# A replanned order, in-place score products and another start in an attention and gated feed-forward block on one core

## The chip, the core and the metric

The kernel runs on one core of one Trainium2 chip. A core has TensorE (PE in the profile; its weight loads are PEld), VectorE (DVE), ScalarE (ACT), GpSimd (POOL) and SyncE (SP), which here issues all DMA transfers. The metric is device time in microseconds, the median of several executions.

## The reference

An input x of 2048 rows by 512 goes through an attention block with a compressed memory and then through a gated feed-forward block, both on a normalised input and both added to their input. Cut to what matters:

```python
# q, k, v: 32 heads of 16; the sequence is 4 segments of L = 512
for s in range(4):
    logits = einsum("bhqd,bhkd->bhqk", qs, ks) * 16**-0.5 + mask  # causal inside a segment
    a_dot = softmax(logits) @ vs
    pq = phi(qs)                               # t + 1 where t > 0, else exp(t)
    a_mem = (pq @ M) / (pq @ z + 1e-6)         # memory of the segments before
    outs.append(g * a_mem + (1 - g) * a_dot)   # g = sigmoid(beta) per head
    M = M + phi(ks).T @ vs ; z = z + phi(ks).sum over rows
h = x + concat(outs) @ wo
out = h + (gelu(ln(h) @ w_gate) * (ln(h) @ w_up)) @ w_down     # 1376 hidden columns
```

The two normalisations are over a row of 512, and everything is in float32.

## The kernel before

Large products are made from a high and a low part of each operand (three matrix products in place of one: high with high, high with low, low with high; `SPLIT`). So each operand that comes from a projection or from memory is split by an ACT copy (high) and a DVE or POOL subtraction (low).

The attention's work is cut into 16 units U: a chunk c of 8 heads in a segment s. A unit projects q and k (`qkv`), splits them, spreads them by DMA into the buffers `stq` and `stk`, updates the memory, and is then handled in two halves Q of 4 heads, 32 in all. `pass_a(Q)` computes the scores once to find each query row's largest score: 11 tiles of up to 512 columns go from PE into one of two PSUM banks (`PA`), and 16 DVE products (`tensor_tensor_reduce` with the mask, a custom operation in the profile, followed by a read of its accumulator) take the minimum of the negated scores. Their element-wise output is not used; it goes into a buffer `junk`. Widths are 128 (i + 1) columns for i = 3, 2, 1, 0, with four products each. The 16 columns of minima are transposed on PE and sent by DMA into a spare row of `stq`, so that the second scores come out with the maximum subtracted. `pass_b(Q)` computes those scores with the keys on the partitions, again into two banks (`PB`), ACT takes the exponential into `pt`, POOL clears what the mask hides, and PE sums the weighted values with products tiled by columns (four at a time).

The order is not written by hand. Every instruction is recorded with its engine, a duration, a priority and what it reads and writes; `Sched.run` then plays a list schedule on these estimates: among what could start within a small window, the lowest priority number goes first. Priorities are the unit's or half's number plus an offset from the table `DUE` (one list per kind of step: `q` projections, `a` and `b` the two passes, `p` the weighted sums, and so on). `LAT` is the time that the planner adds between an instruction's end on one engine and its consumer's start on another; `TAKEN` is the same for a buffer's return. Buffers come from pools (`Pool_`); a pool with `fifo=True` hands them out in the order of the program's text. What comes out is a fixed order of instructions for each engine; on the chip each engine runs through its order and waits by semaphores.

At the start, `ln1(0)` loads four row tiles and normalises them. While DVE finishes the statistics, 17 transposes whose result is unused keep PE at work; then 16 transposes bring the rows into four banks, ACT and DVE split them into `xt`, and the first projections of q and k (`project`) follow. With `ln1(1)`, the first units and their scores join.

After attention, `wo_seg` multiplies with wo and adds x, and the feed-forward block runs over 11 column tiles with products combined after Strassen's scheme (`ffn`, `down`). The change touches none of these functions.

Of the kernel before, what the change touches and what calls it, by code (L numbers as in the profile page):

```python
# [15 lines left out]
P = 128  # L16
D = 512
T = 2048
NSEG = 4
NCH = 4  # L20
ND = D // P
# [10 lines left out]


DUE = {
# [17 lines left out]
}  # L52


# [65 lines left out]
class Op:  # L120
# [2 lines left out]

LAT = {
    "PE": {"PE": 0.0, "ACT": 0.27, "DVE": 0.246, "POOL": 0.24, "SP": 0.25},
    "ACT": {"PE": 0.14, "ACT": 0.12, "DVE": 0.137, "POOL": 0.172, "SP": 0.12},
    "DVE": {"PE": 0.108, "ACT": 0.12, "DVE": 0.17, "POOL": 0.165, "SP": 0.12},
    "POOL": {"PE": 0.085, "ACT": 0.08, "DVE": 0.09, "POOL": 0.12, "SP": 0.12},  # L130
}
TAKEN = {"PE": 0.22, "ACT": 0.14, "DVE": 0.12, "POOL": 0.1}
DRAIN = 0.1


# [106 lines left out]
def infini_geglu(ctx: ExitStack, tc: tile.TileContext, x, wq, wk, wv, wo, beta,  # L242
# [8 lines left out]
    def sb(name, shape, dt=F32):  # L251
        return p0.tile(shape, dt, name=name)

    def many(name, n, shape, dt=F32):
        return [sb(f"{name}{i}", shape, dt) for i in range(n)]
# [14 lines left out]
        return S.op("POOL", dur, prio, fn, ins, outs, **k)  # L270

    def dma(prio, fn, ins, outs, kb=256, dur=None, **k):
        return S.op("SP", dur or (0.4 if kb == 256 else 0.68), prio, fn, ins, outs, lat=kb / 290, **k)

    def mm(n):
        return max(n / 2400 + 0.0133, 0.109)
# [34 lines left out]
    PACC = Pool_([], fifo=True)  # L311
    PGE = Pool_(many("ge", 1, [P, D]))
    PC = Pool_([])
    PPT = Pool_(many("pt", 2, [P, D]), then=PACC)
    PROW1 = Pool_(many("pt1", 9, [P, D]), then=PPT)
    PJ = Pool_(many("junk", 2, [P, D]), then=PC)
    PE_ = Pool_(many("e", 1, [P, D]), then=PC)
    PPQ = Pool_(many("pq", 1, [P, D]), then=PC)
    PPK = Pool_(many("pk", 1, [P, D]), then=PC)
    PPKN = Pool_(many("pkn", 1, [P, D]), then=PC)  # L320
    PPVS = Pool_(many("pvs", 1, [P, D]), then=PGE)
# [7 lines left out]
    PMB = Pool_(many("mb", 7, [P, 160]))  # L329
    PNM = Pool_(many("nm", 2, [P, 2, 2, 4]))  # L330
    PMM = Pool_(many("mm", 2, [P, 2, 2, 8], F32R))
    PMX = Pool_(many("mx", 2, [32, P]))
    PBN = Pool_(many("bn", 2, [P, 4, 6]))
    PMV = Pool_(many("mv", 2, [P, 4, 2]))
    PLN = Pool_(many("ln", 8, [P, 4]))

    ident = sb("ident", [P, P])
    amask = sb("amask", [P, D])
# [1 line left out]
    one = sb("one", [P, 1])  # L340
    gt = sb("gt", [P, 2, NCH])
    tick = sb("tick", [P, 1])
    o_dram = dram.tile([NSEG, 4, P, NCH, P], F32, name="o_dram")
    r_dram = dram.tile([16, 2, 8, D], F32, name="r_dram")
    pv_dram = dram.tile([16, 2, P, D], F32, name="pv_dram")
# [2 lines left out]
    vident, vamask, vmmask, vgt = (Val() for _ in range(4))  # L348


    vh = Val(PJ)
    vj = Val(PJ)


# [101 lines left out]
    def layer_norm(prio, rows, dst, off=False, keep=None, acq=None, done=(), behind=(), scratch=None):  # L456
# [37 lines left out]
        if done and not behind:  # L494

            wm = Val(PB)
            pe(17 * 0.227, prio, lambda: [nc.tensor.transpose(
                wm.t[0:24, 0:P], bn.t.rearrange("p t k -> p (t k)"), ident) for n in range(17)],
                [bn, vident], [wm])

        def g():
# [62 lines left out]
                    op1=OP.mult), [rows[t], mv, y], [rows[t]])  # L564
        if done and not behind:

            pts = [Val(PA if dc == 3 else PD) for dc in range(ND)]
            pe(4 * TR, prio, lambda: [nc.tensor.transpose(
                pts[dc].t[:, t * P:(t + 1) * P], rows[t].t[:, dc * P:(dc + 1) * P], ident)
                for t in range(4) for dc in range(ND)], [*rows, vident], pts, acq=dst)  # L570
            for dc in range(ND):
                split_psum(prio, pts[dc], dst[dc])
            return
# [47 lines left out]
            pe(3 * mm(D), prio, f, [w, XT[s][dc]], [pm], acq=acq)  # L621
        return pm

    def phi(prio, pm, pool_):

        e, r = Val(PE_), Val(pool_)
        act(D, prio, lambda: nc.scalar.activation(e.t, pm.t, AF.Relu, scale=-1.0), [pm], [e],
            acq=[r])
        act(D, prio, lambda: nc.scalar.activation(e.t, e.t, AF.Exp, scale=-1.0), [e], [e],
            src=0.092)  # L630
        dve(D, prio, lambda: nc.vector.scalar_tensor_tensor(
            r.t, pm.t, 0.0, e.t, op0=OP.max, op1=OP.add), [pm, e], [r])
        return r
# [31 lines left out]
    def qkv(U):  # L665
# [5 lines left out]
        moved = prio + DUE["d"][U]  # L671
        for Q in half:
            STQ[Q], STK[Q] = Val(PSQ), Val(PSK)
        for i in range(2):
            hl = Val(PHL)
            if U == 0:
                HL0.append(hl)
            pm = project(first + 0.1 * i, W[s // 2, c, i], s, [hl])
            sc = 0.25 if i == 0 else 1.0
            act(D, first, lambda pm=pm, hl=hl, sc=sc: nc.scalar.activation(  # L680
                hl.t[:, 0], pm.t, AF.Copy, scale=sc), [pm], [hl])
            dve(D, first, lambda pm=pm, hl=hl, sc=sc: nc.vector.scalar_tensor_tensor(  # L682
                hl.t[:, 1], pm.t, sc, hl.t[:, 0].bitcast(F32), op0=OP.mult, op1=OP.subtract),
                [pm], [hl])
            if i == 0 and s:
                PQ[U] = phi(first, pm, PPQ)
            if i == 1 and s < NSEG - 1:
                PQ[U, "k"] = phi(first, pm, PPK)
            for h, Q in enumerate(half):
                dst = (STQ, STK)[i][Q]  # L690
                zeros = (vq0, vk0)[i][Q:Q + 1]
                for r, part in enumerate(((0, 1, 0), (0, 0, 1))[i]):
                    if i == 0:
                        dma(moved + 0.2 + h, lambda dst=dst, r=r, part=part, h=h, hl=hl:
                            nc.sync.dma_start(dst.t[r:P:4].bitcast(F32),
                                              hl.t[64 * h:64 * h + 64, part].bitcast(F32)),
                            [hl] + zeros, [dst], kb=128, chain=True)
                        continue
                    for a in range(2):
                        dma(moved + 0.2 + h, lambda dst=dst, r=r, part=part, h=h, hl=hl, a=a:  # L700
                            nc.sync.dma_start(
                                dst.t[64 * a + r:64 * a + 64:4, :, a].bitcast(F32),
                                hl.t[64 * h + 32 * a:64 * h + 32 * a + 32, part].bitcast(F32)),
                            [hl] + zeros, [dst], kb=64, chain=True)
                if i == 0 and Q >= len(stq_t):
                    dma(moved + 0.2 + h, lambda dst=dst: nc.sync.dma_start(
                        dst.t[3:P:32].bitcast(F32), amask[0:16, 0:2 * P]), [vamask], [dst],
                        kb=16, chain=True)
# [74 lines left out]
    def pass_a(Q):  # L783
# [4 lines left out]
        def part(heads, i):  # L788
# [12 lines left out]
            m = mm(2 * w if i < 2 else w)  # L801
            pe(m * len(heads) / 2 if i < 2 else m, prio, f, [sq, sk], [sa], acq=[nm], tail=m)
            for k, (a, p) in enumerate(heads):
                junk = Val(PJ)

                def g(k=k, a=a, p=p, junk=junk):
                    nc.vector.tensor_tensor_reduce(  # L807
                        out=junk.t[:, :w], in0=sa.t[:, k * w:(k + 1) * w], in1=amask[:, D - w:],
                        op0=OP.add, op1=OP.min, scale=-1.0, scalar=BIG,
                        accum_out=nm.t[:, a, p, i:i + 1])  # L810
                dve(w, prio, g, [sa, vamask], [junk, nm], chain=True)
        for i in (3, 2):
            for n in range(4):
                part([(n % 2, n // 2)], i)
# [23 lines left out]
    def pass_b(Q):  # L838
# [55 lines left out]
        def accum(kbs, last):  # L894
            def f():
                for kb in kbs:
                    for n in range(4):
# [4 lines left out]
                                         e.t[:, lo:lo + D - kb * P], start=kb == 0,  # L902
                                         stop=last and kb == kbs[-1],
                                         tile_position=(0, 32 * n), skip_group_check=True)
            pe(sum(0.02 + 0.86 * (4 - kb) / 4 for kb in kbs), Q + 1.122 + DUE["p"][Q], f,
               [va, *dict.fromkeys(pt[n, kb][0] for kb in kbs for n in range(4))], [pv], head=0.03,
               tail=0.02, mode="c")
        for n in range(4):
# [395 lines left out]
```

## Time and profile before

| | |
|---|---|
| median of 3 runs | 831.09 us (830.61 to 831.82) |
| the profiled execution | 830.79 us, of which the span of the profile is 829.1 us |
| PE | busy 805.0 us, 97% of the span |
| DVE, ACT, POOL | 74%, 68%, 58% busy |
| granted PE clock | 1.00 in the mean of the span |

"L807" is line 807 of the kernel before. In a group's row stand the line, the engine, the operation, output and inputs by the program's names, shapes, the count, then total busy time and the mean duration of one in ns, then the idle time of the engine in front of these instructions and what ended it. Products on PE overlap in the pipeline, so their mean duration (390 ns for 512 columns) is longer than their distance, and a busy PE can still lose time in small gaps.

### The profile page before, as it was taken

The page shows a single profiled execution, that of the slowest core. Times are in us where ns is not written, and L with a number is a line of the kernel's source. Part 1 is how long each engine was busy: PE and PEld are TensorE (multiplying, and loading weights), DVE is VectorE, ACT ScalarE, POOL GpSimd, SP SyncE. Part 2 cuts the span into 40 slices and gives each one's busy share as a digit, 9 for nine tenths or more (in the row PEclk, how much of TensorE's full clock was granted, in tenths as well). Part 3 has the DMA queues.
Part 4 walks back from the last instruction along what each step waited for, and adds up shares of the span by engine and source line. Part 5 has one row for each costly group of instructions (what it writes and reads, how often), then busy time and mean ns, then how long its engine had stood idle before and what let it go on. Part 6 is the DMA issues. An engine that isn't in the chain of part 4 may idle for free.

```text
span 829.1 us, 15346 instructions
## 1 busy us (share of the span) xinstructions
PE 805.0 (97%) x4709; PEld 623.6 (75%) x4709; DVE 612.0 (74%) x1831; ACT 563.5 (68%) x1127; POOL 484.2 (58%) x719
## 2 busy tenths in 40 slices
PE   5999999999999999999999999999999999999998
PEld 4877767777777677776667677777888887788886
DVE  7888678788895878888896874676568856756565
ACT  6877868689988768776776862787467464545551
POOL 7533433444445444544736895788697686778750
PEclk9999999999999999999999999999999999999999
DMA  6543534565456564556554665531111341212102
GB/s 229 148 133 94 153 108 130 151 182 155 118 156 177 159 154 119 154 152 169 165 163 144 200 200 166 164 115 48 55 55 48 95 162 51 65 39 63 51 1 102
DMA packets 71750, 103.52 MB, mean 125 GB/s; under 512 B 14324, under 2 KB 24884, under 8 KB 71668
## 3 DMA queue, kind: packets, MB, share of 16 engines
q1 hardware_dynamic: 71668, 102.54, 42.6%
q8 instruction: 37, 0.61, 0.3%
q14 instruction: 45, 0.37, 0.2%
HBM read 54.92 MB, written 21.43 MB: 92 GB/s over the span
## 4 chain that ended last, share of the span: by engine, by line
PE 77%; DVE 10%; ACT 4%; issue 3%; POOL 3%; DMA 2%; SPq 1%; ACTq 0%; POOLq 0%; DVEq 0%
PE bank L1145 19%; PE bank L1206 14%; PE bank L619 8%; PE bank L797 8%; PE bank L869 7%; PE bank L900 7%; PE bank L973 4%; PE bank L648 4%; DVE junk L807 3%; ACT pt L876 1%; PE bank L726 1%; POOL raw L1122 1%; PE bank L772 1%; PE bank L579 1%; DVE hl L682 1%
## 5 line engine op out<-in xcount | busy, mean ns | idle before, releaser
L807 DVE CUSTOM_DVE_ANT_0 junk<-bank,amask 128x256 f32<-128x256 f32 (+3 forms) x512 | 228.3, 485 | 43.4 <-PE bank L797 40.3
L879 POOL TENSOR_SCALAR_AFFINE_SELECT pt<-pt 128x128 f32<-128x128 f32 (+2 forms) x352 | 118.8, 346 | 191.6 <-ACT pt L876 183.5
L876 ACT ACTIVATE pt<-bank 128x512 f32<-128x512 f32 (+1 forms) x352 | 181.4, 560 | 42.8 <-PE bank L869 36.4
L797 PE MATMUL bank<-stk,stq 128*128 128x512 f32 (+2 forms) x384 | 128.1, 377 | 4.3 <-DVE nm L807 3.9
L869 PE MATMUL bank<-stq,stk 128*128 128x384 f32 (+2 forms) x384 | 110.8, 351 | 1.7 <-ACT pt L876 1.4
L619 PE MATMUL bank<-xt,w 128*128 128x512 f32 x384 | 108.4, 394 | 1.1 <-DVE xt L589 1.1
L1211 DVE TENSOR_TENSOR pt<-pt,bank 128x512 f32<-128x512 f32 x96 | 65.0, 685 | 41.7 <-PE bank L1206 40.1
L797 PEld LDWEIGHTS bank<-stk,stq 128*128 128x128 f32 x384 | 68.6, 188 | 28.4 <-DVE nm L807 13.8
L869 PEld LDWEIGHTS bank<-stq,stk 128*128 128x128 f32 x384 | 67.3, 188 | 19.9 <-ACT pt L876 8.3
L619 PEld LDWEIGHTS bank<-xt,w 128*128 128x128 f32 x384 | 70.4, 188 | 12.5 <-DVE xt L589 1.3
L900 PE MATMUL bank<-pt,vaug 128*32 128x512 f32 (+3 forms) x1024 | 77.0, 436 | 0.0
L900 PEld LDWEIGHTS bank<-pt,vaug 128*32 128x32 f32 x1024 | 28.9, 109 | 39.1 <-issue 30.2
L648 PE MATMUL bank<-wv,xt 128*128 128x256 f32 x384 | 54.9, 283 | 0.0
L648 PEld LDWEIGHTS bank<-wv,xt 128*128 128x128 f32 x384 | 52.2, 189 | 1.8 <-issue 0.2
L1145 PE MATMUL bank<-xt,w 128*128 128x512 f32 (+1 forms) x186 | 51.2, 391 | 0.4 <-DVE n L1171 0.4
L1115 POOL TENSOR_TENSOR w<-raw,w 128x512 fp32r<-128x512 f32 (+3 forms) x37 | 42.0, 1137 | 6.8 <-ACT w L1113 6.6
L435 POOL TENSOR_TENSOR w<-raw,w 128x512 fp32r<-128x512 f32 (+1 forms) x23 | 29.7, 1291 | 22.3 <-ACT w L430 22.1
L807 DVE DVE_READ_ACCUMULATOR2_ANT nm<- 128x1 f32 x512 | 42.0, 82 | 0.0
L1145 PEld LDWEIGHTS bank<-xt,w 128*128 128x128 f32 (+1 forms) x186 | 34.3, 186 | 8.9 <-ACT ge L1163 0.8
L1145 PE MATMUL bank<-stk,w 128*128 128x512 f32 (+1 forms) x138 | 38.8, 390 | 0.0
L1122 POOL TENSOR_TENSOR raw<-raw,raw 128x256 f32<-128x256 f32 (+1 forms) x44 | 35.2, 799 | 2.9
L1122 POOL TENSOR_TENSOR raw<-raw 128x256 f32<-128x256 f32 (+1 forms) x44 | 33.6, 765 | 1.8
(298 smaller groups left out, 1798.5 us busy)
## 6 DMA issues: line engine op xcount, KB each, us to landing
stq<-hl SPq DMA_DIRECT2D x96, 128.0 KB
stk<-hl SPq DMA_DIRECT2D x192, 64.0 KB
pv_dram<-pvs SPq DMA_DIRECT2D x32, 256.0 KB
r<-r_dram SPq DMA_DIRECT2D x28, 256.0 KB
row<-x SPq DMA_DIRECT2D x24, 256.0 KB
raw<-wg SPq DMA_DIRECT2D x20, 256.0 KB
raw<-wu SPq DMA_DIRECT2D x20, 256.0 KB
raw<-wd SPq DMA_DIRECT2D x20, 256.0 KB
```

Of the source, the lines that this page charges most:

```text
L619: nc.tensor.matmul(pm.t, w.t[:, wi, dc * P:(dc + 1) * P], XT[s][dc].t[:, xi, :], start=dc == 0 and n == 0, stop=dc == ND - 1 and n == 2)
L648: nc.tensor.matmul(pm.t[:, 256 * t:256 * t + 256], XT[s][dc].t[:, xi, t0:t0 + P], whl[wi].t[:, h, 256 * (dc % 2):256 * (dc % 2) + 256], st ...
L797: nc.tensor.matmul(sa.t[:, k * w:(k + n) * w].rearrange("x (n w) -> x n w", n=n), sq.t[:, p, i * P:(i + 1) * P], sk.t[:, p, a:a + n, 0:w], ...
L807: nc.vector.tensor_tensor_reduce(out=junk.t[:, :w], in0=sa.t[:, k * w:(k + 1) * w], in1=amask[:, D - w:], op0=OP.add, op1=OP.min, scale=-1 ...
L869: nc.tensor.matmul(sc.t[:, lo:lo + D - q0], sk.t[:, p, a, q0:q0 + P], sq.t[:, p, q0:D], start=True, stop=True)
L876: act(w, prio, lambda: nc.scalar.activation(e.t[:, :w], sc.t[:, :w], AF.Exp), [sc], [e])
L879: nc.gpsimd.affine_select(v, v, pattern=pat + [[1, P]], compare_op=OP.is_ge, fill=0.0, base=0, channel_multiplier=-1)
L900: nc.tensor.matmul(pv.t[32 * n:32 * n + 32, kb * P:D], va.t[:, kb, 17 * j:17 * j + 32], e.t[:, lo:lo + D - kb * P], start=kb == 0, stop=la ...
L1122: pool(0.14 + 2.13e-3 * h, prio, lambda: nc.gpsimd.tensor_tensor(d.t[:, d0:d0 + h], a.t[:, a0:a0 + h], c.t[:, c0:c0 + h], op=o), ins, [d])
L1145: nc.tensor.matmul(dst.t[:w], v.t[:, wi, c0 + j * w:c0 + (j + 1) * w], b[bk][j].t[:, xi, :], start=first and j == 0 and n == 0, stop=j == ...
L1206: nc.tensor.matmul(pm.t, HH[p, f, s][hi].t[:w, t * P:(t + 1) * P], v.t[:w, wi, :], start=f == fl[0] and n == 0, stop=f == fl[-1] and n == 2)
L1211: dve(D, prio, lambda a=a, pm=pm: nc.vector.tensor_tensor(a.t, a.t, pm.t, op=OP.add), [pm], [a])
```

## The change

- In `pass_a`, products of width 512 and 384 (i = 3 and 2) write their unused output over the scores that they read, in the bank. Those of width 256 and 128 write into one small buffer, `aside`. One `junk` buffer goes, and with it the planner's reservation of one per product.
- The number of buffers changes: two for phi(q) in place of one, one transposed maximum (`mx`) in place of two, six small normalisation buffers in place of eight; `pt` buffers are handed out in the text's order; buffers of phi are reserved before the projection.
- The planner's numbers: hand-overs from ACT, DVE and POOL to PE 0.40 us longer, returns of buffers from ACT and DVE 0.10 us longer, the weighted sums' durations and small DMAs' durations changed, and all of `DUE` replaced. These move instructions, and cost nothing by themselves.
- The start: 12 unused transposes in place of 17; the transposed rows go to two banks of `PA`, one of `PB` and one of the three others, and the first two projections (`project_two`) run together, per slice with the high part of x times both weight parts for q and k first, and then the low part.

Each score pass has two banks before and after. Line numbers after the change are higher: the row-maximum products are L825 (L807 before), their scores L817 (L797), pass B's scores L887 and L880 (L869 and L862), its exponential L894 (L876), the weighted sums L918 (L900), projections L621 and, for the first two, L633 (L619).

```diff
 DUE = {
-    "q": [-2.625, -0.25, 3.5, 2.5, 1.75, 1.625, -0.25, 0.875, 0.375, 0.625, 1.75, 1.75, 1.75, 1.625, 3.5, 1],
+    "q": [-4, -4, 1.75, 2.5, 4, -3.75, 2.375, 1.25, 2.25, 4, 1.875, 3.875, 3.5, -3.5, 0.75, 4],
...
-    "w": [0.25, -0.375, -3.5, 3.125],
-    "l": [0, 0, 0.125, -0.25],
+    "w": [1.875, 0.875, -3.375, 4],
+    "l": [0, 0, -1.625, 0.375],
...
-    "ACT": {"PE": 0.14, "ACT": 0.12, "DVE": 0.137, "POOL": 0.172, "SP": 0.12},
-    "DVE": {"PE": 0.108, "ACT": 0.12, "DVE": 0.17, "POOL": 0.165, "SP": 0.12},
-    "POOL": {"PE": 0.085, "ACT": 0.08, "DVE": 0.09, "POOL": 0.12, "SP": 0.12},
+    "ACT": {"PE": 0.54, "ACT": 0.12, "DVE": 0.137, "POOL": 0.172, "SP": 0.12},
+    "DVE": {"PE": 0.508, "ACT": 0.12, "DVE": 0.17, "POOL": 0.165, "SP": 0.12},
+    "POOL": {"PE": 0.485, "ACT": 0.08, "DVE": 0.09, "POOL": 0.12, "SP": 0.12},
...
-TAKEN = {"PE": 0.22, "ACT": 0.14, "DVE": 0.12, "POOL": 0.1}
+TAKEN = {"PE": 0.22, "ACT": 0.24, "DVE": 0.22, "POOL": 0.1}
...
-    PPT = Pool_(many("pt", 2, [P, D]), then=PACC)
+    PPT = Pool_(many("pt", 2, [P, D]), fifo=True, then=PACC)
...
-    PJ = Pool_(many("junk", 2, [P, D]), then=PC)
+    PJ = Pool_(many("junk", 1, [P, D]), then=PC)
...
-    PPQ = Pool_(many("pq", 1, [P, D]), then=PC)
+    PPQ = Pool_(many("pq", 2, [P, D]), then=PC)
...
-    PMX = Pool_(many("mx", 2, [32, P]))
+    PMX = Pool_(many("mx", 1, [32, P]))
...
-            pe(17 * 0.227, prio, lambda: [nc.tensor.transpose(
-                wm.t[0:24, 0:P], bn.t.rearrange("p t k -> p (t k)"), ident) for n in range(17)],
+            pe(12 * 0.21, prio, lambda: [nc.tensor.transpose(
+                wm.t[0:24, 0:P], bn.t.rearrange("p t k -> p (t k)"), ident) for n in range(12)],
...
-            pts = [Val(PA if dc == 3 else PD) for dc in range(ND)]
+            pts = [Val(pool_) for pool_ in ((PA, PA, PB, PD) if not behind else (PD, PD, PD, PA))]
...
+    def project_two(prio, w, s, acq):
+        pm = [Val(PD), Val(PD)]
+        for dc in range(ND):
+            def f(dc=dc):
+                for n, (i, wi, xi) in enumerate((i, wi, xi) for wis, xi in (((0, 1), 0), ((0,), 1))
+                                                for i in range(2) for wi in wis):
+                    nc.tensor.matmul(pm[i].t, w[i].t[:, wi, dc * P:(dc + 1) * P], XT[s][dc].t[:, xi, :],
+                                     start=dc == 0 and n in (0, 2), stop=dc == ND - 1 and n > 3)
+            pe(6 * mm(D), prio, f, [*w, XT[s][dc]], pm, acq=acq if dc == 0 else [])
+        return pm
...
             for k, (a, p) in enumerate(heads):
-                junk = Val(PJ)
-
-                def g(k=k, a=a, p=p, junk=junk):
+                def g(k=k, a=a, p=p):
                     nc.vector.tensor_tensor_reduce(
-                        out=junk.t[:, :w], in0=sa.t[:, k * w:(k + 1) * w], in1=amask[:, D - w:],
+                        out=sa.t[:, :w] if i > 1 else aside[:, k * w % 256:k * w % 256 + w], in0=sa.t[:, k * w:(k + 1) * w], in1=amask[:, D - w:],
                         op0=OP.add, op1=OP.min, scale=-1.0, scalar=BIG,
                         accum_out=nm.t[:, a, p, i:i + 1])
-                dve(w, prio, g, [sa, vamask], [junk, nm], chain=True)
+                dve(w, prio, g, [sa, vamask], [nm], chain=True)
...
-            pe(sum(0.02 + 0.86 * (4 - kb) / 4 for kb in kbs), Q + 1.122 + DUE["p"][Q], f,
+            pe(sum(0.735 * (4 - kb) / 4 for kb in kbs) + (0.17 if last else 0.06), Q + 1.122 + DUE["p"][Q], f,
```

More of the change, by code (lines that the diff above doesn't have):

```diff
@@ L272, in dma @@
     def dma(prio, fn, ins, outs, kb=256, dur=None, **k):
-        return S.op("SP", dur or (0.4 if kb == 256 else 0.68), prio, fn, ins, outs, lat=kb / 290, **k)
+        return S.op("SP", dur or (0.4 if kb == 256 else 0.64), prio, fn, ins, outs, lat=kb / 290, **k)
     def mm(n):
@@ L331, in infini_geglu @@
     PMM = Pool_(many("mm", 2, [P, 2, 2, 8], F32R))
[L332 removed]
+    PMX = Pool_(many("mx", 1, [32, P]))
     PBN = Pool_(many("bn", 2, [P, 4, 6]))
     PMV = Pool_(many("mv", 2, [P, 4, 2]))
[L335 removed]
+    PLN = Pool_(many("ln", 6, [P, 4]))
     ident = sb("ident", [P, P])
@@ L342, in infini_geglu @@
     tick = sb("tick", [P, 1])
+    aside = sb("aside", [P, 2 * P])
     o_dram = dram.tile([NSEG, 4, P, NCH, P], F32, name="o_dram")
@@ L348, in infini_geglu @@
     vident, vamask, vmmask, vgt = (Val() for _ in range(4))
-    vh = Val(PJ)
+    vh = Val(PE_)
     vj = Val(PJ)
@@ L622, in project, with phi @@
         return pm
-    def phi(prio, pm, pool_):
-        e, r = Val(PE_), Val(pool_)
+    def project_two(prio, w, s, acq):
[8 more added lines that the diff above has]
+        return pm
+    def phi(prio, pm, r):
+        e = Val(PE_)
         act(D, prio, lambda: nc.scalar.activation(e.t, pm.t, AF.Relu, scale=-1.0), [pm], [e],
@@ L673, in qkv @@
             STQ[Q], STK[Q] = Val(PSQ), Val(PSK)
+        hls = Val(PHL), Val(PHL)
+        if U == 0:
+            first_two = project_two(first, [W[0, 0, 0], W[0, 0, 1]], 0, hls)
         for i in range(2):
-            hl = Val(PHL)
+            hl = hls[i]
             if U == 0:
                 HL0.append(hl)
-            pm = project(first + 0.1 * i, W[s // 2, c, i], s, [hl])
+            if i == 0 and s:
+                PQ[U] = Val(PPQ)
+            if i == 1 and s < NSEG - 1:
+                PQ[U, "k"] = Val(PPK)
+            r = PQ.get((U, (U, "k"))[i])
+            pm = project(first + 0.1 * i, W[s // 2, c, i], s, [hl] + ([r] if r else [])) if U else first_two[i]
             sc = 0.25 if i == 0 else 1.0
@@ L684, in qkv @@
                 [pm], [hl])
[L685 to L688, printed above, removed]
+            if r:
+                phi(first, pm, r)
             for h, Q in enumerate(half):
```

28 rows, old and new, of the table DUE are left out of this document.

## The prediction

> **What bounds the kernel now.** First the head of the profile page, for the engine that is full.
>
> ```profile
> span 829.1 us, 15346 instructions
> PE 805.0 (97%) x4709; PEld 623.6 (75%) x4709; DVE 612.0 (74%) x1831; ACT 563.5 (68%) x1127; POOL 484.2 (58%) x719
> ```
>
> TensorE (PE) is busy for 805.0 of 829.1 us, so 24.1 us is all that it idles outright, and the change takes no matrix product away: in the order of the built programs the same 4,072 products stand in both, beside 17 warm-up transposes before and 12 after. What can change is the start, and the small waits inside the "busy" 97%. The windows view tells where these are.
>
> ```profile
> core 0: us, PE busy (x) PEld busy (x) DVE busy (x) ACT busy (x) POOL busy (x), PEclk, DMA share, GB/s
> 20.00:100.00 80.00, 78.57 (x548) 61.49 (x548) 65.29 (x258) 65.51 (x137) 33.74 (x67) 1.00 0.49 132
> 100.00:400.00 300.00, 295.20 (x2106) 222.18 (x2108) 242.23 (x955) 235.58 (x501) 136.09 (x297) 1.00 0.54 149
> 400.00:480.00 80.00, 76.13 (x489) 52.63 (x482) 66.03 (x215) 60.09 (x121) 53.22 (x88) 1.00 0.58 177
> ...
> 560.00:829.00 269.00, 264.36 (x1173) 215.08 (x1172) 172.81 (x266) 141.00 (x254) 185.52 (x179) 1.00 0.21 64
> ```
>
> The feed-forward part (from about 480 us) loses almost nothing: 1.7% idle in its last window, and that holds the output's way out behind the last product. Attention loses PE time in crumbs, with VectorE (DVE) at about 81% of each of its stretches. The view of waits says for whom PE's weight loads (PEld) and its products wait.
>
> ```profile
> PEld bank L900 <- issue: 30.2, 121, 0.4
> PEld bank L797 <- DVE nm L807: 13.8, 32, 1.7
> PEld bank L869 <- ACT pt L876: 8.3, 24, 1.0
> ...
> PEld bank L900 <- POOL pt L879: 7.0, 28, 0.4
> ...
> PEld bank L830 <- DVE pk L631: 2.4, 3, 1.6
> PEld bank L862 <- ACT pt L876: 2.3, 5, 0.9
> PEld bank L830 <- DVE mm L826: 1.6, 4, 0.5
> ...
> PE bank L797 <- DVE nm L807: 3.9, 8, 0.8
> PE bank L869 <- ACT pt L876: 1.4, 3, 0.5
> ```
>
> The columns are total us, times, longest. Score products (L797, L869, L862) wait for a bank whose last reader, a row-maximum product on DVE or an exponential on ACT, isn't done. [...]
>
> **The start.** The chain that ended last, over the first 20 us:
>
> ```profile
> 7.61 3.58 PE bank L497 x17
> 11.19 1.43 PE bank L568 x13
> ...
> 13.27 0.70 DVE xt L589
> ...
> 14.02 5.08 PE bank L619 x21
> ```
>
> and from the timeline and the view of line 497 (durations min/median/max in ns, first and last start):
>
> ```profile
> 9.80 1.45 DVE L533 TENSOR_SCALAR pt<-pt,mv,ln 128x512 f32<-128x512 f32 x3
> 9.92 0.82 ACT L545 ACTIVATE pt<-pt,ln,ln 128x512 f32<-128x512 f32 x1 [0.52 <-DVE ln L539]
> ...
> 12.64 2.07 ACT L588 ACTIVATE xt<-bank 128x512 fp32r<-128x512 f32 x4 [1.91 <-PE bank L568]
> ...
> L497 PE MATMUL bank<-ident,bn x17: 273/421/421, 7.6 to 10.9; 128*24 128x128 f32 x17
> ```
>
> The 17 warm-ups take 3.58 / 17 = 0.21 us each, and hold the real transposes (L568, 1.43 / 13 = 0.11 us each) until about 11.1. The first normalised row is there at 9.80 + 0.48 = 10.3, the third at 11.25, ACT's fourth at 10.74. With 12 warm-ups PE is free by 7.6 + 12 x 0.21 = 10.1, so the last eight transposes hang on the third row: 11.25 + 0.1 + 8 x 0.11 = 12.2, against 11.19 + 1.43 = 12.6. That is 0.4 us. Then the projection: before, its first product waits for the low part (L589, done at 13.97), because it uses the bank that L589 reads and PE takes a slice's three products together. After, two free banks and the order "high part times both weight parts, for q and k, then the low part" let PE start behind the first L588, at about 12.2 + 0.6 + 0.1 = 12.9 instead of 14.0. From there 24 products at 5.08 / 21 = 0.24 us set the pace: per slice four high products take 0.96 us, longer than L588's 2.07 / 4 = 0.52. Start and end of the projections come 1.1 us earlier. Some may be lost to the value weights, split by ACT and POOL; some is won since SP's order now sends the first head's six key parts without a weight load between them. I take **-1.2** (ends 0 and -2).
>
> **The wide products over their scores.** 256 of the 512 row-maximum products (512 and 384 columns) now write into the bank they read; the narrow ones write into one buffer. No run here shows this operation so; the nearest rows are an add from bank to bank and the same add into on-chip memory:
>
> ```profile
> L807 DVE CUSTOM_DVE_ANT_0 junk<-bank,amask 128x512 f32<-128x512 f32 x128 | 85.9, 683 | 13.1 <-PE bank L797 12.3
> L807 DVE CUSTOM_DVE_ANT_0 junk<-bank,amask 128x384 f32<-128x384 f32 x128 | 67.7, 551 | 20.7 <-PE bank L797 19.6
> ...
> L1157 DVE TENSOR_TENSOR bank<-vaug,bank 128x512 f32<-128x512 f32 x22 | 15.2, 693 | 11.7 <-PE bank L1145 8.4 <-ACT vaug L1152 3.2
> ...
> L1157 DVE TENSOR_TENSOR vaug<-vaug,bank 128x512 f32<-128x512 f32 x9 | 6.2, 687 | 1.3 <-PE bank L1145 1.3
> ```
>
> 693 - 687 = 6 ns more each: 256 x 6 ns = 1.5 us of DVE, spread under its 19% idle time. Some 32 of 512 products are waited for, so PE sees 1.5 x 32 / 512 = **+0.1** us; at -6 to +60 ns each it would be -0.1 to +1. The bank is released by the same instruction as before. The freed buffer goes to a second phi(q) buffer; one transposed-maximum buffer instead of two costs nothing, since its DMA leaves before the next maximum, on average 13 us of PE work later.
>
> **The turns of PE.** The order has 65 runs of column-tiled products after, 62 before, so 129 turns against 123: 6 x 0.25 (30.2 / 121) = **+1.5** us (ends 0 and 2.4).
>
> **The new order.** The waits that a better order can remove are those on DVE and ACT: 13.8 + 8.3 + 2.4 + 2.3 + 1.6 = 28.4 us in 68 waits, 0.42 us each. Not all is lost time, as the product in front still streams while a load waits; PE's own rows show 3.9 + 1.4 = 5.3 us idle outright. Between 5 and 28 us I take the middle, 17 us. How much goes is read from the order, with each product at its pace in the trace, as PE work between two instructions. The distance at which a score bank is reused was under 1.4 us (product 0.68, two hand-overs and the rest) for 126 of 351 pass-A tiles and 175 of 351 pass-B tiles; after, 100 and 140, a fifth fewer. From a maximum's transpose to the first pass-B product the median goes from 7.5 to 10.1 us, from the key transpose to the memory update from 1.7 to 2.9, from the last score product to the last weighted sum from 2.6 to 2.95. All grow while PE's work stays the same, so no length is paid for it. The planner's hand-overs to PE got 0.40 us longer, as long as the mean wait. A fifth by the counts, more by the mean: I take a third of 17 us, **-6** (ends 0 and -17, and above nothing by the second rival).
>
> Sum: -1.2 + 0.1 + 1.5 - 6 = -5.6 us. The profiled execution took 830.8 us (its span 829.1 and 1.7 around it), 0.3 under the median of 831.1; the forecast stands to the median: 831.1 - 5.6 = **825.5 us**.
>
> **Rivals.**
> 1. *The waits only move* (no real change): other tiles wait in place of these, as the longest singles (1.7, 1.6, 1.0 us) come from a full DVE queue, which a margin doesn't empty. Left are -1.2 + 0.1 + 1.5 = +0.4: 831.5 us. For: DVE has the same work. Against: all distances grew.
> 2. *DVE falls behind in clumps* (slower). With DVE's instructions at their durations, the seven fullest stretches of 20 us of PE work in attention carry 27, 27, 25, 24, 24, 23 and 22 us after, 25, 25, 24, 23, 23, 22 and 22 before: 8 us more. If PE has other work ready for half of it, that is +4 us, and with the other terms 831.1 + 4 + 0.4 = 835.5 us. It decides where a stretch holds over 23 us of DVE work, more than DVE can do in the 21.5 us that PE then really takes; I count six after, four before. Against: PE's work between two maxima spreads no worse (standard deviation 3.0 against 2.9 us).
> 3. *All waits under 0.4 us go*, as every margin holds: about 13 of the 17 us; 831.1 - 13 + 0.4 = 818.5 us, and 814.5 if all 17 go.
> 4. *The clock is late.* PE's pace went from 0.21 to 0.11 us a transpose within the last warm-ups (the shortest of them has 273 ns, the others 421), so after about 3.2 us, at 10.8. Twelve last 2.5 us, and a pause of 0.2 us follows. If full pace then comes one such stretch later, at about 14, 16 transposes at +0.1 and five products at +0.23 us cost 1.6 + 1.1 = 2.7: 828.2 us with the rest as forecast. For keeping the time: the transposes that follow keep PE at work across 10.8. [...]
>
> **How the numbers follow.** About 0.2% (1.7 us) is what a measurement of this kernel can tell from no change. Chances: forecast (821 to 829.4) 0.48, rival 3 0.12, rival 4 0.08, rival 1 0.10, rival 2 0.22. Faster are the forecast and rivals 3 and 4, 0.68; same is rival 1 with its edge towards slower, 0.09; slower 0.23. The range holds the forecast's ends, rivals 1, 3 and 4 down to 815, and the nearer half of rival 2: 815 to 836. The forecast's own range is 820 to 829.
>
> **What would show it.** Right: first projection product near 12.9 us; the waits of L797's and L869's successors on DVE and ACT at two thirds of 22.1 us together; wide products at 690 and 557 ns; L900's successor with some 127 "issue" waits. Wrong: projections starting at 13.5 or later at 0.4 us a product (the clock); those waits unchanged (rival 1); DVE's idle time before the wide products, 13.1 + 20.7 = 33.8 us now, down to 24 with PE waiting more (rival 2).

## The result and the profile after

The changed kernel takes **835.57 us** (834.05 to 835.94) against 831.09 us (830.48 to 831.82): slower by 4.5 us, a ratio of 1.0051 with a 95% interval of 1.0037 to 1.0066. The forecast was 825.5.

First the head of the page of the changed kernel, then rows of its view of waits (total us, times, longest).

```profile
span 833.7 us, 15303 instructions
PE 810.5 (97%) x4704; PEld 625.8 (75%) x4704; DVE 619.1 (74%) x1831; ACT 564.4 (68%) x1127; POOL 484.2 (58%) x719
```

```profile
PEld bank L918 <- issue: 34.1, 136, 0.4
PEld bank L817 <- DVE nm L825: 15.3, 43, 1.0
PEld bank L918 <- POOL pt L897: 5.9, 20, 0.6
PEld bank L887 <- ACT pt L894: 5.0, 12, 0.9
PEld bank L880 <- ACT pt L894: 2.8, 6, 1.3
PE bank L817 <- DVE nm L825: 3.1, 8, 0.5
```

PE's outright idle time did not grow (24.1 us before, 833.7 - 810.5 = 23.2 now): what was lost lies inside its busy share, where a weight load waits while the product in front still counts as busy. The waits of pass B on ACT did get shorter (8.3 + 2.3 before, 5.0 + 2.8 now). Those of pass A on DVE grew from 32 to 43 in number and from 13.8 to 15.3 us, and the waits on nothing at the weighted sums from 121 to 136. Where DVE's time went is seen in its groups by form, the changed kernel's first, then two rows of the kernel before that the prediction does not show, its 256-column products and the reads:

```profile
L825 DVE CUSTOM_DVE_ANT_0 bank<-bank,amask 128x512 f32<-128x512 f32 x128 | 87.1, 699 | 12.0 <-PE bank L817 11.7
L825 DVE CUSTOM_DVE_ANT_0 bank<-bank,amask 128x384 f32<-128x384 f32 x128 | 70.6, 575 | 20.0 <-PE bank L817 19.1
L825 DVE DVE_READ_ACCUMULATOR2_ANT nm<- 128x1 f32 x512 | 56.9, 111 | 0.0
L825 DVE CUSTOM_DVE_ANT_0 aside<-bank,amask 128x256 f32<-128x256 f32 x128 | 54.2, 423 | 14.3 <-PE bank L817 8.9
```

```profile
L807 DVE CUSTOM_DVE_ANT_0 junk<-bank,amask 128x256 f32<-128x256 f32 x128 | 48.0, 420 | 5.3 <-PE bank L797 4.5
L807 DVE DVE_READ_ACCUMULATOR2_ANT nm<- 128x1 f32 x512 | 42.0, 82 | 0.0
```

Two things stand out. A 256-column product still takes 420 ns, but DVE now idles 14.3 us in front of these products in place of 5.3, and only 8.9 of it is PE's. And the accumulator read behind a product has a mean of 111 ns in place of 82. The timeline shows the first of these in one group of products, DVE of the kernel before and then of the changed one (start, duration):

```profile
101.37 0.42 DVE L807 CUSTOM_DVE_ANT_0 junk<-bank,amask 128x256 f32<-128x256 f32 x1
101.72 0.09 DVE L807 DVE_READ_ACCUMULATOR2_ANT nm<- 128x1 f32 x1
101.72 0.42 DVE L807 CUSTOM_DVE_ANT_0 junk<-bank,amask 128x256 f32<-128x256 f32 x1
102.06 0.08 DVE L807 DVE_READ_ACCUMULATOR2_ANT nm<- 128x1 f32 x1
```

```profile
108.61 0.14 DVE L825 DVE_READ_ACCUMULATOR2_ANT nm<- 128x1 f32 x1
108.61 0.42 DVE L825 CUSTOM_DVE_ANT_0 aside<-bank,amask 128x256 f32<-128x256 f32 x1
108.96 0.08 DVE L825 DVE_READ_ACCUMULATOR2_ANT nm<- 128x1 f32 x1
109.08 0.42 DVE L825 CUSTOM_DVE_ANT_0 aside<-bank,amask 128x256 f32<-128x256 f32 x1
109.42 0.09 DVE L825 DVE_READ_ACCUMULATOR2_ANT nm<- 128x1 f32 x1
109.66 0.42 DVE L825 CUSTOM_DVE_ANT_0 aside<-bank,amask 128x256 f32<-128x256 f32 x1
```

Before, the next product starts together with the read of the one in front, 0.35 us after that one's start. After, it starts only when the read is over and a little later, 0.47 and 0.58 us on. The 256-column products all write the columns 0 to 255 of `aside`, so each must see the last one's writes done: in the built program 108 of the 256 narrow products wait on DVE's own semaphore for the read of the product just in front, where before only one did (the others wait there, if at all, for a product further back, which is done by then).

Between neighbours the median distance went from 345 to 468 ns (86 pairs of 256 columns) and from 360 to 577 ns (20 pairs of 256 to 128). The first median mixes two kinds: 61 pairs at 467 ns with this wait alone, and 25 at 577 where the product also carries a wait for PE, as all 20 of the other pairs do. By the two medians DVE takes 86 x 0.123 + 20 x 0.217 = 14.9 us more; by the kinds it is at most 61 x 0.122 + 25 x 0.232 + 20 x 0.217 = 17.6 us, as some of these products would have waited for PE anyway. So the estimate is some 15 to 18 us. The 128-column ones lie at 0 and 128 in turn and kept 211 ns.

That is **theory A**: the shared buffer lost the 4.5 us and what the rest might have gained. Its rivals: the wide products' write into the bank (the longer read, theory B), the late clock (theory C), the new order itself.

### The profile page after: what moved, and what is told of

The parts are those of the page before. It is cut to its first block, busy times and chain, and to the rows that moved or that the text cites. A ratio compares the mean times of both kernels' runs of the same rounds, so it can differ in the third digit from the quotient of the medians.

```text
span 833.7 us, 15303 instructions
## 1 busy us (share of the span) xinstructions
PE 810.5 (97%) x4704; PEld 625.8 (75%) x4704; DVE 619.1 (74%) x1831; ACT 564.4 (68%) x1127; POOL 484.2 (58%) x719
## 4 chain that ended last, share of the span: by engine, by line
PE 46%; DVE 6%; POOL 2%; ACT 1%; DMA 1%; issue 1%; SPq 0%; DVEq 0%; POOLq 0%; ACTq 0%
PE bank L1163 22%; PE bank L1224 14%; PE bank L991 4%; PE bank L817 1%; PE bank L918 1%; PE bank L887 1%; DVE aside L825 1%; POOL raw L1140 1%; DVE bank L825 1%; PE bank L621 1%; DVE row L564 1%; DVE bank L1020 1%; DMA cd<-pv_dram 1%; PE bank L581 0%; DMA raw<-wu 0%
## 5 line engine op out<-in xcount | busy, mean ns | idle before, releaser
L894 ACT ACTIVATE pt<-bank 128x512 f32<-128x512 f32 (+1 forms) x352 | 182.7, 558 | 42.4 <-PE bank L887 30.0
L825 DVE CUSTOM_DVE_ANT_0 bank<-bank,amask 128x512 f32<-128x512 f32 (+1 forms) x256 | 156.6, 637 | 32.0 <-PE bank L817 30.9
L817 PE MATMUL bank<-stk,stq 128*128 128x512 f32 (+2 forms) x384 | 132.9, 387 | 5.1 <-DVE nm L825 3.1
L887 PE MATMUL bank<-stq,stk 128*128 128x384 f32 (+2 forms) x384 | 113.3, 351 | 1.5 <-ACT pt L894 1.4
L621 PE MATMUL bank<-xt,w 128*128 128x512 f32 x360 | 102.8, 395 | 0.0
L825 DVE CUSTOM_DVE_ANT_0 aside<-bank,amask 128x256 f32<-128x256 f32 (+1 forms) x256 | 83.7, 355 | 19.1 <-PE bank L817 11.0
L817 PEld LDWEIGHTS bank<-stk,stq 128*128 128x128 f32 x384 | 68.9, 188 | 32.4 <-DVE nm L825 15.3
L887 PEld LDWEIGHTS bank<-stq,stk 128*128 128x128 f32 x384 | 68.1, 189 | 19.1 <-issue 6.7
L918 PE MATMUL bank<-pt,vaug 128*32 128x512 f32 (+3 forms) x1024 | 76.7, 436 | 0.0
L621 PEld LDWEIGHTS bank<-xt,w 128*128 128x128 f32 x360 | 65.2, 188 | 10.0 <-DVE xt L591 0.2
L918 PEld LDWEIGHTS bank<-pt,vaug 128*32 128x32 f32 x1024 | 28.7, 109 | 40.9 <-issue 34.1
L825 DVE DVE_READ_ACCUMULATOR2_ANT nm<- 128x1 f32 x512 | 56.9, 111 | 0.0
L437 POOL TENSOR_TENSOR w<-raw,w 128x512 fp32r<-128x512 f32 x25 | 32.2, 1291 | 30.2 <-ACT w L432 22.1
L1163 PE MATMUL bank<-xt,w 128*128 128x512 f32 (+1 forms) x168 | 46.4, 394 | 0.0
L1133 POOL TENSOR_TENSOR stk<-raw,stk 128x512 fp32r<-128x512 f32 (+3 forms) x28 | 31.0, 1110 | 23.3 <-PE bank L1163 14.5
L1163 PE MATMUL bank<-xt,stk 128*128 128x512 f32 (+1 forms) x138 | 38.1, 391 | 0.2 <-ACT pq L1170 0.2
```

The lines of the kernel that those rows point to most:

```text
L621: nc.tensor.matmul(pm.t, w.t[:, wi, dc * P:(dc + 1) * P], XT[s][dc].t[:, xi, :], start=dc == 0 and n == 0, stop=dc == ND - 1 and n == 2)
L817: nc.tensor.matmul(sa.t[:, k * w:(k + n) * w].rearrange("x (n w) -> x n w", n=n), sq.t[:, p, i * P:(i + 1) * P], sk.t[:, p, a:a + n, 0:w], ...
L825: nc.vector.tensor_tensor_reduce(out=sa.t[:, :w] if i > 1 else aside[:, k * w % 256:k * w % 256 + w], in0=sa.t[:, k * w:(k + 1) * w], in1= ...
L887: nc.tensor.matmul(sc.t[:, lo:lo + D - q0], sk.t[:, p, a, q0:q0 + P], sq.t[:, p, q0:D], start=True, stop=True)
L894: act(w, prio, lambda: nc.scalar.activation(e.t[:, :w], sc.t[:, :w], AF.Exp), [sc], [e])
L918: nc.tensor.matmul(pv.t[32 * n:32 * n + 32, kb * P:D], va.t[:, kb, 17 * j:17 * j + 32], e.t[:, lo:lo + D - kb * P], start=kb == 0, stop=la ...
```

## The experiments

Ratios are against the kernel before, run in turn on the same chip, with 95% intervals. Every kernel but the one with other due times keeps the PE order of the kernel it is made from.

**The changed kernel with 17 warm-ups** (theory C).

```diff
-                wm.t[0:24, 0:P], bn.t.rearrange("p t k -> p (t k)"), ident) for n in range(12)],
+                wm.t[0:24, 0:P], bn.t.rearrange("p t k -> p (t k)"), ident) for n in range(17)],
```

> The changed kernel with 17 unused transposes at the start in place of 12; every other instruction stands where it stood. Theory C (the late clock): in the changed kernel the clock opened at 13.4 us instead of 10.8, the sixteen transposes took 0.21 us each, and the first projection began at 14.1 instead of 12.9. Here it should begin at 12.9 to 13.1, and the end comes 1.2 to 2 us earlier: 833.6 to 834.4 us against 835.6. If the start does not carry to the end (a later wait hides it): 835.6 as before.

836.94 us, 1.0053 [1.0036, 1.0069], where 833.6 to 834.4 was expected. The transposes ran at full pace (273 ns) from the third on and the projections started at 13.4 in place of 14.1 us, and the end did not come earlier. Theory C does not explain the 4.5 us. The test isn't clean for a smaller gain: in its profile PE is 0.7 us ahead of the changed kernel to 150 us and 0.7 behind from 300 us on, and the granted clock then fell to half for 3.4 and 6.8 us (0.83 in the mean from 420 to 430 us, 0.77 from 460 to 475), which it did not in the profile of the changed kernel. The two executions with a mean clock of 0.998 and 1.0 took 833.81 and 834.93 us, the four at 0.993 to 0.996 took 836.7 to 838.8. Whether 17 warm-ups are worth up to 1 us stays open.

**The narrow products in two halves in turn** (theory A). The buffer is bf16, so that it keeps its size.

```diff
-    aside = sb("aside", [P, 2 * P])
+    aside = sb("aside", [P, 4 * P], mybir.dt.bfloat16)
...
-out=sa.t[:, :w] if i > 1 else aside[:, k * w % 256:k * w % 256 + w]
+out=sa.t[:, :w] if i > 1 else aside[:, k * w % 512:k * w % 512 + w]
```

> The changed kernel, in which the narrow row-maximum products' unused output goes to two halves of the small buffer in turn (in bfloat16, so that the buffer keeps its size; that output is read by nobody). Same order on every engine. Theory A (the shared buffer): in the changed kernel each narrow product waits for the one before, because both write the same columns: 468 ns from one 256-wide product to the next in place of 345, 577 ns from a 256-wide to a 128-wide one in place of 360. That is some 16 us of VectorE time in the 32 halves. Here the distances return to 345 and 360, and the end comes 3 to 5 us earlier: 831 to 832.5 us. Theory B (the new order itself is the slower one): distances return, the time does not: 835 us or more.

830.18 us (828.80 to 832.22), 0.9982 [0.9972, 0.9992]: 1.4 us ahead of the kernel before in the same series, where the changed kernel was 4.5 us behind it in its own. That is 5.9 us between the two. Its groups and waits:

```profile
L825 DVE CUSTOM_DVE_ANT_0 aside<-bank,amask 128x256 bf16<-128x256 f32 x128 | 48.0, 419 | 10.8 <-PE bank L817 10.2
```

```profile
PEld bank L918 <- issue: 32.4, 129, 0.4
PEld bank L817 <- DVE nm L825: 10.0, 30, 0.9
PEld bank L887 <- ACT pt L894: 8.6, 23, 0.9
```

The distance of 345 ns is back, the product's own mean is the same in bf16 (419 ns against 423), and the scores wait 10.0 us for DVE in place of 15.3. Theory A holds in this order.

**Both edits together.**

```diff
-... for n in range(12)],
+... for n in range(17)],
...
-out=sa.t[:, :w] if i > 1 else aside[:, k * w % 256:k * w % 256 + w]
+out=sa.t[:, :w] if i > 1 else aside[:, k * w % 512:k * w % 512 + w]
```

> The changed kernel with both: 17 unused transposes, and the narrow products' unused output in two halves in turn. Theories A and C together: 829.5 to 831 us, at or a little under the kernel before. Theory B: still 3 us or more above it, 834 us.

831.37 us, 1.0001 [0.9990, 1.0012], 0.4 us above what was expected. Five more warm-ups bring nothing here either; in this profile too the granted clock fell to half, for 6.8 us from 459 us on.

**The order before, only the wide products in place** (theory B).

```diff
-                        out=junk.t[:, :w], in0=sa.t[:, k * w:(k + 1) * w], in1=amask[:, D - w:],
+                        out=sa.t[:, :w] if i > 1 else junk.t[:, :w], in0=sa.t[:, k * w:(k + 1) * w], in1=amask[:, D - w:],
```

> The kernel before, in its own order, with only the 512- and 384-wide products writing over their scores; the narrow ones keep the two buffers. In the changed kernel the read of the accumulator behind a wide product took 141 ns in place of 83, so the score bank is free 58 ns later, while the distance to the next product stayed at 610 ns. If that release counts: +0.5 to +1.5 us, 831.6 to 832.6 us. If only the distance of the products counts: 831.1 us, no change.

831.99 us, 1.0006 [0.9996, 1.0016]: at most 1.3 us, and not clear of nothing. The read behind a wide product takes 141 ns here too, while wide products still start as far apart as before (616 and 483 ns).

**The order before, only the narrow products together**: theory A without the new order, as every engine keeps the order of the kernel before.

```diff
-    PJ = Pool_(many("junk", 2, [P, D]), then=PC)
+    PJ = Pool_(many("junk", 2, [P, D]), then=PC); PJ.first = PJ.free[0][2]
...
-                        out=junk.t[:, :w], in0=...
+                        out=junk.t[:, :w] if i > 1 else PJ.first[:, k * w % 256:k * w % 256 + w], in0=...
```

> The kernel before, with its own order on every engine, in which only the narrow row-maximum products (256 and 128 columns) write into one buffer, at the same columns as in the changed kernel; the wide ones keep their two buffers in turn. The theory that the shared buffer is what the change loses by: distances from product to product grow as in the changed kernel (256 to 256 from 345 to some 468 ns, 256 to 128 from 360 to some 577 ns), some 16 us more of DVE time in the whole, and the end comes 4 to 6 us later: 835 to 837 us. Rival, that only the new order has too little room for it: the distances grow the same, but the time stays within 1.5 us of the kernel before, 831 to 833 us.

841.32 us, 1.0101 [1.0088, 1.0114]: 8.3 us slower than the kernel before, more than expected.

```profile
L807 DVE CUSTOM_DVE_ANT_0 junk<-bank,amask 128x256 f32<-128x256 f32 x128 | 54.1, 423 | 9.7 <-PE bank L797 2.3
```

```profile
PEld bank L797 <- DVE nm L807: 21.9, 48, 1.7
PE bank L797 <- DVE nm L807: 6.0, 15, 0.8
```

With nothing moved, the scores' waits on DVE go from 13.8 + 3.9 to 21.9 + 6.0 us. DVE's idle 19% did not absorb it. Instruction by instruction, PE falls behind the kernel before all through attention, from 1.2 us at 20 us to 9.5 at 440, and hardly more after that (9.9 at the end). (In this profile 1.0 us of the loss is the start's, where the clock rose 5.3 us after the first warm-up in place of 3.2.) The test is somewhat harder than the changed kernel: the one buffer is also one of the two that the wide products write. In 9 of 22 places a 256-column product now also waits for a 384-column one in front (some 710 ns apart in place of 483), and in 6 of 12 a 512-column one for a 128-column one (438 in place of 228). With them DVE takes at most some 22 us more, not 18, which goes with a loss above the 4 to 6 us expected.

**The kernel before with 12 warm-ups.**

```diff
-... for n in range(17)],
+... for n in range(12)],
```

> The kernel before with 12 warm-up transposes in place of 17, and nothing else. The clock theory: the clock opens at about 13.4 us in place of 10.8, all 16 transposes run at 0.21 us, the first projection starts no earlier than 14.0, and the time is unchanged or up to 0.5 us longer: 831.0 to 831.6 us. The prediction's own working, that fewer warm-ups let the transposes come 0.4 us earlier, would give 830.7 us with the first projection still at 14.0, since the low part of x holds it here.

831.13 us, 0.9983 [0.9969, 0.9997]. Both expectations miss the ratio. The clock was not late:

```profile
L568 PE MATMUL bank<-ident,pt x16: 272/273/473, 10.3 to 12.4; 128*128 128x128 f32 x16
```

Only the first few transposes were slow. But its work runs within 0.9 us of the kernel before at every point from 20 to 820 us (PE work done, from the first warm-up), so the profile has no 1.9 us to show; the kernel before stood at 833.03 us in this series against 831.1 and 831.6 in others. What made this ratio stays open; that fewer warm-ups cost something is not seen.

**Other due times for the output products**, in the version with narrow products apart.

```diff
-    "w": [1.875, 0.875, -3.375, 4],
+    "w": [0.25, -0.375, -3.5, 3.125],
```

> The changed kernel with the narrow products apart, and with the due times of the output products (the table's row w) of the kernel before, which moves the last attention half behind the last normalisation's transposes, where the other order has only 16 weighted-sum runs there. Theory of the hand-over: the order by 150 us is 2 to 3 us ahead of the kernel before and loses it between 340 and 480 us, where PE waits for the last normalisation (2.4 us by its rows) and runs thin enough for the granted clock to fall for some us. With products left to run beside that normalisation the loss is smaller, and the end is 1 to 2.5 us ahead of the version with narrow products apart: 827.5 to 829 us. Rival: what the hand-over lost was only brought forward by the good stretch, any order meets it, and the time stays at 830 to 831 us; or another wait takes its place, and it is slower than the kernel before.

843.75 us, 1.0129 [1.0116, 1.0142]. The windows of this kernel around the hand-over (PE, PEld, DVE, ACT, POOL busy, clock, DMA):

```profile
450.00:460.00 10.00, 9.43 (x57) 5.59 (x56) 9.79 (x44) 8.48 (x17) 4.64 (x12) 1.00 0.17 55
460.00:470.00 10.00, 5.33 (x29) 3.47 (x28) 9.89 (x18) 7.10 (x13) 7.05 (x7) 0.83 0.32 84
470.00:480.00 10.00, 8.45 (x23) 5.49 (x23) 2.25 (x4) 7.63 (x17) 4.83 (x11) 0.66 0.42 132
```

DVE is full from 450 to 470 us with the last row maxima and the last normalisation together, and PE, with nothing else ready, stands idle for 4.7 of ten. The remedy made the hand-over worse: another wait took the place of the one it aimed at, as the last clause of the expectation has it. That a thin PE lowers the granted clock was the author's estimate and is not shown: here the clock went to 0.83 and 0.66 behind 5.33 busy us in ten, and with both edits to 0.71 behind 9.06, but in the changed kernel, with 7.72 from 460 to 470 us, it stayed at 1.00. The hand-over does depend on the order, but this edit does not show that the new order had lost its gain there.

**All products outside the bank**: narrow ones apart, and wide ones into two bf16 halves of the remaining junk buffer (theory B in the new order).

```diff
-    PJ = Pool_(many("junk", 1, [P, D]), then=PC)
+    PJ = Pool_(many("junk", 1, [P, D]), then=PC); wide = PJ.free[0][2].bitcast(mybir.dt.bfloat16)
...
-out=sa.t[:, :w] if i > 1 else aside[:, k * w % 512:k * w % 512 + w]
+out=wide[:, a * D:a * D + w] if i > 1 else aside[:, k * w % 512:k * w % 512 + w]
```

> The version with the narrow products apart, in which the wide ones too write outside the bank, into two bf16 halves of the one junk buffer in turn, with the order unchanged on every engine. The theory that the write into the bank costs by the accumulator read behind it: the read falls from 141 to some 83 ns, the bank is free some 58 ns earlier, 256 products save 15 us of DVE, and since about one product in ten is waited for, the end comes 0.5 to 1.5 us earlier than with narrow products apart alone: 828.7 to 829.7 us. Rival, that the in-place write costs nothing, as the starts of two products in a row stand as far apart as before: no change, 830 to 830.5 us.

830.69 us, 0.9985 [0.9974, 0.9996]. The reads are short again and the time is that of the narrow products apart (0.9982 in another series), so theory B's gain of 0.5 to 1.5 us does not come (the junk buffer is ACT's scratch in the normalisations too, which makes a few wide products wait 2 to 3 us in all):

```profile
L825 DVE DVE_READ_ACCUMULATOR2_ANT nm<- 128x1 f32 x512 | 42.0, 82 | 0.0
```

**Only the wide products outside**, the narrow ones as in the changed kernel.

```diff
-out=sa.t[:, :w] if i > 1 else aside[:, k * w % 256:k * w % 256 + w]
+out=wide[:, a * D:a * D + w] if i > 1 else aside[:, k * w % 256:k * w % 256 + w]
```

> The changed kernel in which only the wide products write outside the bank (two bf16 halves of the junk buffer in turn); the narrow ones still share the columns of one buffer, and the order is unchanged. If the narrow products' shared buffer is the loss, and the wide ones' place is nearly none of it, this stays at 834 to 835.5 us with the distances of the changed kernel (256 to 256 at 468 ns); if the in-place write were the loss, it would return to 829 to 831 us. Against the version with all products apart it should be 5 to 6 us slower.

834.78 us, 1.0028 [1.0016, 1.0039]: 4.1 us slower than with all products outside, on the same chip in the same series, where 5 to 6 were expected. (The time lies in the range expected only because the kernel before stood at 832.56 us in this series.)

```profile
PEld bank L817 <- DVE nm L825: 16.8, 47, 1.1
```

So the shared buffer alone costs about 4 us here too (some of it may be the junk buffer's: wide products wait 4.3 us for ACT's use of it, against 2.5 with all products outside). Against the changed kernel's 1.0051, taken in another series, the wide products' place may be worth up to 2 us where DVE is already late; the two intervals overlap, so it isn't settled.

## Why the prediction was wrong

The waits of PE's weight loads from 20 to 480 us, all rows of the view of waits added up by the engine waited for, give the account (us; the last column compares the medians of a series):

| | on DVE | on ACT | on nothing or POOL | time against before |
|---|---|---|---|---|
| before | 22.9 | 12.0 | 49.4 | |
| changed | 29.4 | 8.8 | 53.4 | +4.5 |
| changed, narrow apart | 19.3 | 11.9 | 55.5 | -1.4 |
| changed, all outside the bank | 21.8 | 10.0 | 53.5 | -1.9 |
| changed, only wide outside | 27.7 | 9.7 | 53.5 | +2.2 |
| before, narrow together | 31.5 | 11.3 | 50.8 | +8.3 |

**The step that failed: the wide products' term, where it says "the narrow ones write into one buffer" and prices nothing.** It costed what the edit does to the 256 wide products and left the other 256 without a row. The sharing takes some 15 to 18 us of DVE time in the new order. It is worth 4.1 and 5.9 us there, and +8.3 us in the order before, where 20 more products wait for the one in front. Each time the weight loads' waits on DVE change with it: 22.9 to 31.5, 21.8 to 27.7, 19.3 to 29.4. Without it the sign of the forecast was right: 0.9982 [0.9972, 0.9992]. It is not the whole miss: of 835.57 - 825.5 = 10.1 us it is 5.9 by the version with narrow products apart, and the other 4.2 us are that all the remaining terms together came to -1.4 us there, not -5.6. Most of that is the new order's -6, taken up below.

**Wide products, +0.1.** Right in size where the narrow ones are apart: no difference with and without the bank in the new order, +0.4 in the old. Its row did mislead: a plain add between banks is not followed by a read (none behind the 66 of L1157), and here the product took 16 to 24 ns more (6 forecast) and the read behind it 141 ns in place of 83. Since two products in a row start as far apart as before, the read costs DVE nothing; only the bank comes free about 58 ns later.

**The start, -1.2.** Not won in the profile of the changed kernel: first projection at 14.14 where 12.9 was forecast and 14.02 measured before.

```profile
L499 PE MATMUL bank<-ident,bn x12: 373/421/421, 7.6 to 9.9; 128*24 128x128 f32 x12
L570 PE MATMUL bank<-ident,pt x16: 273/417/473, 10.4 to 13.5; 128*128 128x128 f32 x16
L633 PE MATMUL bank<-xt,w x24: 389/389/499, 14.1 to 19.5; 128*128 128x512 f32 x24
```

The transposes have a median of 417 ns where 273 was the full pace: the granted clock rose only at 13.4, as rival 4 said ("at about 14"). That the 12 warm-ups made it late is not shown: with the same 12 it rose 3.3 to 5.8 us after the first of them, from run to run. Rival 4's price of 2.7 us was too high: the first projection lost 14.14 - 12.9 = 1.2 us. In the version with all products outside, the clock rose 3.3 us after the first warm-up:

```profile
L499 PE MATMUL bank<-ident,bn x12: 370/418/418, 8.1 to 10.4; 128*24 128x128 f32 x12
L633 PE MATMUL bank<-xt,w x24: 389/389/500, 13.4 to 18.8; 128*128 128x512 f32 x24
```

There the first projection comes 13.4 - 8.1 = 5.3 us after the first warm-up, against 6.4 before: the 1.1 us of the forecast, where the clock allows it. It did not reach the end: with 17 warm-ups in place of 12 the profiles are 0.7 and 0.6 us ahead to 150 and 200 us, and neither median is lower.

**The turns, +1.5.** No run shows 0.25 us as the price of a turn between full and column-tiled products. Of the 121 waits that give it, 110 stand between the weight loads of four weighted sums and those of the next four, with no other product's load between them (at 203.77 and 204.20 us, for example), and only 11 at the first load of such a row; in the changed kernel it is 115 and 21 of 136. The sum came out too small as well: at the weighted sums the waits on nothing and on POOL's `pt` went from 149 to 156, seven more where six were forecast, and from 37.2 to 40.0 us (2.8 more, not 1.5). But waits on nothing grew at other lines too, so that all of them together gained 4.0 us in the changed kernel, 4.1 with all products outside and 6.1 with the narrow ones apart. Pass B's show it, from 3.3 us in 10 (pass A's fell from 5.6 to 2.5) to

```profile
PEld bank L887 <- issue: 6.7, 19, 0.4
```

**The new order, -6.** With the narrow products apart the waits on DVE and ACT together fall by 3.7 us (34.9 to 31.2), with all outside by 3.1, where 6 was forecast. The waits on nothing and on POOL grew by 6.1 and 4.1 us meanwhile. These sums include waits that a running product covers, so they do not add up to the time: in the new order they stand 2.8 to 4.4 us higher against before than the times do. They suggest why an order with longer distances ends up only 0.15 to 0.18% ahead; no run takes these waits away, so that is argued and not shown. That its early lead is lost at the hand-over to the feed-forward part was argued from the traces and is not shown either.

**The rivals.** Rival 2's 835.5 us is the measured time, but not by its mechanism, so the match is luck, and so is that the range of 815 to 836 holds it. DVE did become the one waited for, by 15 to 18 us of new own waits and not by clumps of the same work; the sign that it named, DVE's idle time before the wide products falling from 33.8 to 24 us, did not come (12.0 + 20.0 = 32.0), and the same order with the narrow products apart is not late. Of the signs of the forecast, the waits of both passes' scores on DVE and ACT in the two main rows stand at 15.3 + 5.0 = 20.3 us, not two thirds of 22.1, the wide products at 699 and 575 ns, not 690 and 557, and the "issue" waits of L918 at 136, not 127.

## What to carry to other kernels

An output that nobody reads still orders its writers (here 108 of 256 products wait for the one in front, and those of 256 columns start 467 or 577 ns apart in place of 345): before unused outputs share a buffer, look in the built order for waits of an engine on itself, and price each by the distance from start to start, not by the duration in the group's row, which didn't move here (420 and 423 ns). Price the part of an edit that "just goes aside" with a row of its own. An engine that is 74% busy may have no spare time in the stretch where another engine waits for it: here 15 to 18 us more of it cost 4 to 6 us of the end, and some 22 us cost 8.

## What the runs showed of the hardware

- **A wait of DVE on itself.** A product that does not wait for the 256-column one in front starts 345 ns after it, though that one is recorded with 420 ns. With the wait it is 467 ns, and 577 ns where it waits for PE's semaphore as well, whether the next is 256 or 128 columns wide. So the wait costs 0.12 us here, and at most 0.23 us together with PE's.
- **The accumulator read** takes 83 ns behind a product that wrote to on-chip memory and 141 ns behind one that wrote into a bank, in both orders.
- **The clock.** The granted clock rose between 3.2 and 5.8 us after the first warm-up: 3.3, 3.7, 4.8, 4.9, 5.8 and 5.8 with 12 of them, and 3.2, 3.8, 3.8, 3.9 and 5.3 with 17. The ranges overlap, and eleven profiles show no clear relation with the number. From one change of the granted clock to the next it is 819.2 us at full clock in the kernel before and in the changed one, and 3.41, 6.83 and 10.24 us at half clock in the middle of the two runs with 17 warm-ups in the new order and of the one with other due times: 240, 1, 2 and 3 times 3.413 us. In the two with 17 warm-ups, PE was still busy for 2.5 to 2.7 us of the last 3.4 to 3.7 us before each such fall. What sets these moments is not shown.
